# Linear attention and two MLPs: the first MLP layer by layer, its second layer by seven products

## The chip, the cores and the metric

The kernel runs on one core of a Trainium2 chip. The metric is the time of one execution on the device in microseconds; shown are the median of several runs and one profiled execution. The engines are TensorE (PE; its weight loads are shown apart as PEld), VectorE (DVE), ScalarE (ACT), GpSimd (POOL) and SyncE (SP), which issues all of the kernel's DMA transfers.

## The reference

All data are float32. Attention has 8 batches, 8 heads, 576 positions and heads of 64; its output, 4608 tokens by 512, goes through two MLPs (512 to 2048 to 512).

```python
def _attn_ref(q, k, v):
    q_s = q - np.max(q, axis=-1, keepdims=True)
    q_s = np.exp(q_s)
    q_s = q_s / (np.sum(q_s, axis=-1, keepdims=True) + 1e-09)
    k_s = k - np.max(k, axis=2, keepdims=True)
    k_s = np.exp(k_s)
    k_s = k_s / (np.sum(k_s, axis=2, keepdims=True) + 1e-09)
    kv = np.einsum('bhsd,bhse->bhde', k_s, v)
    return np.einsum('bhsd,bhde->bhse', q_s, kv)
# x = attention, as tokens by 512
# first MLP:  h = x @ w_in; x = np.maximum(0.01 * h, h) @ w_out
# second MLP: h = x @ w_in; out = (h / (1 + np.exp(-h))) @ w_out
```

## The kernel before, in words

**Precision.** TensorE multiplies in float32r. To keep accuracy each operand is split in a high part (a rounded copy, ScalarE) and a low part (the rest, VectorE, `sub`), and a product is three matmuls: high by high, high by low, low by high.

**Tiling.** Tokens go in 9 blocks `j` of 512 (`TB`), the inner dimension of an MLP in 16 row blocks `f` of 128. A unit of attention is one pair of heads and one block: 36 units `n`, four for each block. `k_task`, `v_task` and `q_task` load a unit, take the maxima and exponentials, form k times v in `kv` (L554, L555) and x for one quarter of the inner dimension (L690). k's maximum over positions needs a transpose, q's softmax another. Units below `DT` = 14 transpose on TensorE (L522, L528, L675, then a copy out of PSUM), later ones on VectorE in pieces of 32 by 32 (L498 to L514; 16 pieces for q, L665).

**First MLP.** Both layers run fused. `layer1` makes one row block of one block of tokens (12 matmuls of 512 columns, L723 to L725), `act` applies the leaky ReLU (L750) and splits the result into a g tile, and `layer2_all` adds its share to four accumulators in PSUM (12 matmuls, L782), which stay for a whole block. Both layers' weights are decoded by `split1` (two ScalarE and four VectorE instructions and a split for each piece) while the first two blocks run, and stay in SBUF. The first two blocks are done in halves (`chunks`).

**Second MLP.** It runs layer by layer, and each layer multiplies blocks of 2 by 2 with seven products in place of eight. A product is 12 matmuls of 256 columns. Layer 1 (`layer1_2`, L1005) does seven products per block of tokens and group `i` of four row blocks, `blocks` puts them together, `active` applies the SiLU, and the results go to DRAM (`gd`). Layer 2 (`layer2_2`, L1054) fetches them (`g_all`) and sums over the four groups in seven PSUM banks. Operands of a product are loaded, some are sums of others (`SUMS`), and each is split (`operand`: `fetch`, `sums`, `split2`). `weights1` and `weights2` do that with the weights, which `convert2` and `convert3` decoded and put into DRAM. x operands live in 12 buffers (`r_x`), seven for each set; the weights in 28.

**What sets the order.** The program is written by a planner (`Queues`): each task is a generator that offers its next instruction with an estimated cost and waits for buffers (`get`) and events (`wait`). The planner takes what can start first, and among equals the lowest rank. Every engine and SyncE's queue then run in that order and wait by semaphores.

**PSUM.** Eight banks: four accumulators (`pacc`), two for layer 1 (`r_h`), two for attention (`r_attn`). The second MLP takes all eight (`r_b`).

Of the kernel before, what the change touches and what calls it, by code (L numbers as in the profile page):

```python
# [202 lines left out]
def linear_attention_two_mlps(  # L203
# [37 lines left out]
    DT = 14  # L241
    NE = 7
    NX = 6
    FS = 6
    NU = 7
    NS = 8

# [8 lines left out]
    pacc = ctx.enter_context(tc.tile_pool(name="pacc", bufs=1, space=PSUM))  # L256
    ph = ctx.enter_context(tc.tile_pool(name="ph", bufs=2, space=PSUM))
# [24 lines left out]
    r_attn = Slots(qs, [lambda i=i: pa.tile([P, TB], F32, tag=f"a{i}", name="a") for i in range(2)])  # L282
# [3 lines left out]
    r_g = Slots(qs, gbuf)  # L286
    r_o = Slots(qs, [outp.tile([P, TB], F32, name=f"o{i}") for i in range(4)])
    r_x = Slots(qs)
    r_b = Slots(qs)
    r_k = ring(atp, [P, 640], F32, "k", 1)  # L290
    q_tiles = [atp.tile([P, TB], F32, name=f"q{i}") for i in range(3)]
    r_q = Slots(qs, q_tiles)
    kx_tile = atp.tile([P, 2, TB], F32, tag="kx", name="kx")
    r_kx = Slots(qs, [kx_tile[:, i] for i in range(2)])
    r_m = ring(sp, [P, 2, D], F32, "m1", 2)
# [12 lines left out]

    wtiles = {}
    spare = {}  # L310
# [43 lines left out]
    def parts_of(f):  # L354

        return ((0,), (1,)) if f < NE else ((0, 1),)

    def w_tag(f, os):
        return f"w{f}" if len(os) == 2 else f"w{f}_{os[0]}"

    def split1(f, os):

        if f == NF - 1:
            yield wait(("l2", 0, 3))
        if f > NF - NU:
            yield wait(("unit", NF - f))
        for e in range(NX):
            if f == NF - NU - e // 2:
                yield wait(("w", 0, 0, e), ("w", 0, 1, e))
        n = DM * len(os)  # L370
        raw = wp.tile([P, 2 * n], U32, tag=w_tag(f, os), name="r" + w_tag(f, os))
        for i, o in enumerate(os):
            yield from load_bits(raw[:, 2 * i * DM:2 * (i + 1) * DM], 0, o, f)
        if f < NX:

            if f // 2 not in spare:
                spare[f // 2] = wp.tile([P, 4, DM], F32, tag=f"w{NF - NU - f // 2}", name=f"t{f}")
            at = 2 * (f % 2) + os[0]
            t = spare[f // 2][:, at:at + len(os)].rearrange("p o n -> p (o n)")
        else:  # L380
            t = yield get(r_raw)
        yield from decode(raw, t[:, 0:n], n)
        w = wp.tile([P, len(os), 2, DM], F32R, tag=w_tag(f, os), name=w_tag(f, os))
        for i, o in enumerate(os):
            wtiles[0, o, f] = w[:, i]
        t2 = t[:, 0:n].rearrange("p (o n) -> p o n", n=DM)
        yield op(("A", a_(n)))
        copy("A", w[:, :, 0], t2)
        yield op(("V", v_tt(n)))
        sub("V", w[:, :, 1], t2, w[:, :, 0])  # L390
        if f >= NX:
            r_raw.put(t)
        for o in os:
            done(("w", 0, o, f))

    def convert2():

        yield wait(("l2", 2, NF - 1))
        for f in range(NF):
            raw = yield get(r_raw)  # L400
            bits = raw.bitcast(U32)
            yield from load_bits(bits, 1, 0, f)
# [4 lines left out]
            nc.sync.dma_start(out=w2d[f], in_=t[:, 0:DM])  # L407
            yield wait()
            r_raw.put(t)
            done(("w2", f))  # L410

    def convert3():

        yield wait(*(("w2", f) for f in range(NF)), ("l2", NB - 1, NF - 1))
        n = DM // 2
        for r in range(NF // 2):
            yield rank(step2(0, r, 0) - 4)
# [26 lines left out]
    def w_of(l, o, f):  # L444
        return wtiles[l, o, f].rearrange("p t (k m) -> p t k m", k=KD)


    kv = {}
    early = {}

    def early_tiles(n):

        if n not in early:
            w = wp.tile([P, 4 * DM], F32, tag=f"w{NF - n}", name=f"u{n}")
            early[n] = w[:, 0:640], w[:, 640:640 + 5 * NV], w[:, 1536:2048]
            nc.vector.memset(early[n][1].rearrange("p (c n) -> p c n", c=5)[:, :, 2 * D:], 1.0)
        return early[n]

    def k_task(n):

        b, j, p = units[n]
        first = 0 < n < NU
        if first:
            kf, vv, _ = early_tiles(n)
        else:
            kf, vv = (yield get(r_k)), vbuf
        ktile = kf
# [25 lines left out]
        if n >= DT:  # L493

            mt = yield get(r_m)
            mtf = mt.rearrange("p h d -> p (h d)")
            yield op(("V", 0.21))
            nc.vector.transpose(out=mtf, in_=m1f)  # L498
            yield op(("V", 0.21))
            nc.vector.tensor_reduce(  # L500
                out=sk[:, 0:4], in_=mtf.rearrange("p (a t) -> p a t", a=4), axis=AX.X, op=ALU.max
            )
            r_m.put(mt)
            for i in range(4):
                yield op(("V", 0.08))
                nc.vector.tensor_copy(out=sk[0:32, 4 + 4 * i:8 + 4 * i], in_=sk[32 * i:32 * i + 32, 0:4])
            yield op(("V", 0.09))
            nc.vector.tensor_reduce(
                out=sk[0:32, 20:24], in_=sk[0:32, 4:20].rearrange("p (i a) -> p a i", i=4),
                axis=AX.X, op=ALU.max, negate=True,  # L510
            )
            for i in range(4):
                yield op(("V", 0.21))
                nc.vector.transpose(  # L514
                    out=m1f[32 * i:32 * i + 32].rearrange("p (a d) -> p a d", a=4),
                    in_=sk[0:32, 20:24].unsqueeze(2).to_broadcast([32, 4, 32]),
                )
            nb = m1f
        else:
            pm = yield get(r_attn)  # L520
            yield op(("p", 0.12))
            nc.tensor.transpose(pm[:, 0:P], m1f, ident)  # L522
            r_m.put(m1)
            nm = small[n % 2]["k"][:, 0:1]
            yield op(("V", v_tt(128)))
            nc.vector.tensor_reduce(out=nm, in_=pm[:, 0:P], axis=AX.X, op=ALU.max, negate=True)
            yield op(("p", 0.12))
            nc.tensor.transpose(pm[:, P:2 * P], nm.to_broadcast([P, P]), ident)  # L528
            nb = pm[:, P:2 * P]
# [8 lines left out]
        if n >= DT:  # L538
            r_m.put(m1)
        else:  # L540
            r_attn.put(pm)
# [14 lines left out]
        if not first:  # L556
            r_k.put(ktile)
# [50 lines left out]
    def q_task(n):  # L608

        b, j, p = units[n]  # L610
        if n > DT:
            yield wait(("qt", n - 1))
# [545 lines left out]
```

## Time and profile before

| | |
|---|---|
| median of 3 runs | 1666.81 us (1665.66 to 1667.26) |
| profiled execution | 1667.91 us, its span 1666.1 us |
| busy: PE, PEld, DVE | 1623.2, 1447.5, 1132.0 us |
| busy: ACT, POOL | 766.4, 65.3 us |
| DMA | 194.71 MB, mean 117 GB/s |

Attention and the first MLP take the span up to about 945 us, the second MLP's first layer lasts until about 1300 us and its second to the end. A shown matmul lasts longer than the distance to the next one, as they overlap; a busy TensorE can so still be fed late. In groups of rows, "idle before" is the engine's idle time just before these instructions.

### The profile page before, as it was taken

How to read it: one execution, taken by the hardware profiler on the slowest of the kernel's cores; microseconds unless marked ns; L12 is line 12 of the kernel's file. 1: busy time of each engine (PE TensorE's matmuls, PEld its weight loads, DVE VectorE, ACT ScalarE, POOL GpSimd, SP SyncE). 2: the span in 40 equal slices, each digit the busy share in tenths (PEclk: the TensorE clock that was granted, in tenths of full speed). 3: DMA queues.
4: the chain of work that ended last, by engine and by line, in shares of the span. 5: the costliest groups of instructions: out<-in, count | busy, mean ns of one | idle time of the engine just before them, and what ended most of it. 6: DMA issues, size and time to landing. Idle time of an engine off the chain costs nothing.

```text
span 1666.1 us, 27003 instructions
## 1 busy us (share of the span) xinstructions
PE 1623.2 (97%) x10036; PEld 1447.5 (87%) x10036; DVE 1132.0 (68%) x2277; ACT 766.4 (46%) x1671; POOL 65.3 (4%) x74
## 2 busy tenths in 40 slices
PE   5899999999999999999999999999999999999999
PEld 3678888787877878887888999999999999999999
DVE  7988337657586784714124798888878877777775
ACT  5687454334353543423233545444446544444442
POOL 2200001101011010000000000000000000000000
PEclk9999999999999999999999999999999999999999
DMA  8741213113233321100021455555548644444442
GB/s 246 259 136 40 78 49 106 36 53 97 73 96 101 110 75 46 45 8 31 1 64 45 139 186 203 195 176 185 174 149 265 190 127 135 134 133 135 136 135 83
DMA packets 170883, 194.71 MB, mean 117 GB/s; under 512 B 53504, under 2 KB 120064, under 8 KB 170752
## 3 DMA queue, kind: packets, MB, share of 16 engines
q1 hardware_dynamic: 170752, 192.99, 37.5%
q8 instruction: 79, 1.29, 0.3%
q14 instruction: 52, 0.43, 0.1%
HBM read 122.68 MB, written 70.25 MB: 116 GB/s over the span
## 4 chain that ended last, share of the span: by engine, by line
PE 82%; DVE 11%; ACT 3%; DMA 2%; issue 1%; SPq 0%; POOL 0%; DVEq 0%; POOLq 0%; ACTq 0%
PE acc L782 18%; PE b L1054 11%; PE c L1054 11%; PE b L1005 11%; PE c L1005 10%; PE h L723 6%; PE h L724 6%; PE h L725 6%; DVE q L665 3%; PE a L690 1%; PE a L554 1%; ACT q L646 1%; DVE g L300 1%; DVE m L514 1%; DVE x L300 1%
## 5 line engine op out<-in xcount | busy, mean ns | idle before, releaser
L782 PE MATMUL acc<-g,w 128*128 128x512 f32 x1728 | 430.1, 395 | 0.4 <-ACT o L304 0.4
L782 PEld LDWEIGHTS acc<-g,w 128*128 128x128 f32 x1728 | 321.4, 188 | 71.7 <-issue 2.1
L300 DVE TENSOR_TENSOR g<-h,g 128x512 fp32r<-128x512 f32 x144 | 99.5, 691 | 243.5 <-ACT g L304 242.5
L723 PE MATMUL h<-x,w 128*128 128x512 f32 x576 | 234.7, 407 | 10.4 <-DVE g L300 7.9
L724 PE MATMUL h<-x,w 128*128 128x512 f32 x576 | 226.6, 393 | 1.6 <-DVE x L300 1.6
L725 PE MATMUL h<-x,w 128*128 128x512 f32 x576 | 226.2, 393 | 0.0
L304 ACT ACTIVATE g<-h 128x512 fp32r<-128x512 f32 x144 | 86.0, 597 | 149.3 <-PE acc L782 148.5
L750 ACT ACTIVATE h<-h 128x512 f32<-128x512 f32 x144 | 84.0, 583 | 143.4 <-PE h L725 140.2
L723 PEld LDWEIGHTS h<-x,w 128*128 128x128 f32 x576 | 108.8, 189 | 43.1 <-DVE g L300 14.1
L1054 PE MATMUL c<-s,x 128*128 128x256 f32 x1056 | 138.7, 283 | 0.4 <-DVE x L300 0.4
L1005 PE MATMUL b<-x,s 128*128 128x256 f32 x1056 | 137.0, 283 | 0.0
L1054 PEld LDWEIGHTS c<-s,x 128*128 128x128 f32 x1056 | 132.0, 192 | 0.6 <-DVE x L300 0.6
L1005 PE MATMUL c<-x,s 128*128 128x256 f32 x1008 | 131.8, 283 | 0.5 <-DVE o L940 0.5
L1005 PEld LDWEIGHTS b<-x,s 128*128 128x128 f32 x1056 | 131.3, 192 | 0.1
L724 PEld LDWEIGHTS h<-x,w 128*128 128x128 f32 x576 | 108.9, 189 | 25.7 <-DVE x L300 3.4
L725 PEld LDWEIGHTS h<-x,w 128*128 128x128 f32 x576 | 108.9, 189 | 23.9 <-DVE w L300 0.7
L1005 PEld LDWEIGHTS c<-x,s 128*128 128x128 f32 x1008 | 125.7, 192 | 0.7 <-DVE o L940 0.7
L1054 PE MATMUL b<-s,x 128*128 128x256 f32 x960 | 125.5, 283 | 0.0
L1054 PEld LDWEIGHTS b<-s,x 128*128 128x128 f32 x960 | 119.7, 192 | 0.0
L304 ACT ACTIVATE x<-x 128x512 fp32r<-128x512 f32 x110 | 69.4, 631 | 109.2 <-DMA x<-gd 76.7
L665 DVE STREAM_TRANSPOSE q<-q 32x128 f32<-32x128 f32 x352 | 106.4, 302 | 11.0 <-PE a L690 3.6
L646 ACT ACTIVATE q<-q,q 128x64 f32<-128x64 f32 x176 | 59.5, 342 | 51.8 <-DVE q L625 51.4
(228 smaller groups left out, 2308.2 us busy)
## 6 DMA issues: line engine op xcount, KB each, us to landing
x<-gd SPq DMA_DIRECT2D x92, 256.0 KB, 2.7
gd<-left SPq DMA_DIRECT2D x75, 256.0 KB, 2.6
gd<-o SPq DMA_DIRECT2D x41, 256.0 KB, 2.7
x2d<-o SPq DMA_DIRECT2D x34, 256.0 KB, 2.1
g<-gd SPq DMA_DIRECT2D x34, 256.0 KB, 2.8
rw<-in_moe_w_in_dram SPq DMA_DIRECT2D x16, 512.0 KB, 4.7
rw<-in_moe_w_out_dram SPq DMA_DIRECT2D x16, 512.0 KB, 5.8
raw<-in_moe_w_in_dram SPq DMA_DIRECT2D x16, 512.0 KB, 4.1
```

What stands on the lines that cost most here:

```text
L300: engines[e].tensor_tensor(out=out_, in0=a, in1=b.bitcast(F32), op=ALU.subtract)
L304: nc.scalar.activation(out=out_, in_=in_, func=ACTF.Copy)
L514: nc.vector.transpose(out=m1f[32 * i:32 * i + 32].rearrange("p (a d) -> p a d", a=4), in_=sk[0:32, 20:24].unsqueeze(2).to_broadcast([32, 4 ...
L646: nc.scalar.activation(out=x4[:, c, h], in_=q4[:, c, h], func=ACTF.Exp, bias=nq[:, at:at + 1], accum_out=sq[:, to:to + 1],)
L665: nc.vector.transpose(out=qT[32 * o:32 * o + 32].rearrange("p (c t) -> p c t", c=4)[:, :, 32 * i:32 * i + 32], in_=q4[32 * i:32 * i + 32, ...
L723: nc.tensor.matmul(h, lhsT=w[:, 0, kk], rhs=x[:, 0], start=kk == 0, stop=False)
L724: nc.tensor.matmul(h, lhsT=w[:, 0, kk], rhs=x[:, 1], start=False, stop=False)
L725: nc.tensor.matmul(h, lhsT=w[:, 1, kk], rhs=x[:, 0], start=False, stop=kk == KD - 1)
L750: nc.scalar.activation(out=h, in_=h, func=ACTF.Prelu, alpha=0.01)
L782: nc.tensor.matmul(a, lhsT=lhsT, rhs=rhs, start=f == first and i == 0, stop=f == last - 1 and i == 2)
L1005: nc.tensor.matmul(bank[:, r * HB:(r + 1) * HB], lhsT=w4[:, a, r, k], rhs=x3[:, b, k], start=n == 0, stop=n == 5,)
L1054: nc.tensor.matmul(bank[:, m * HB:(m + 1) * HB], lhsT=g[:, a, at:at + P], rhs=w[:, b, r * HB:(r + 1) * HB], start=i + m + n == 0, stop=i = ...
```

## The change

- The first MLP runs layer by layer as well. `layer0` makes layer 1 of all nine blocks; `act` now writes the leaky ReLU's result to SBUF, subtracts in even row blocks the first half of the tokens from the second (an operand of the products), and stores the block in DRAM (`gd1`).
- Its second layer is the same function as the second MLP's second layer (`layer_k(1)`): seven products, weights and x swapped as stationary and moving operand, results to `x2d` by `store1`.
- `w_out` of the first MLP is no longer decoded at the start by `split1` but later by `convert1`, into DRAM; `weights1` makes its operands. `convert2` and `convert3` start later.
- All units transpose on TensorE; VectorE's transposes are gone.
- Six sets of buffers for k and v (they take the room of weights that come later), six for q; four PSUM banks for attention and four for layer 1; 16 buffers `r_o`.

```diff
-    DT = 14
-    NE = 7
-    NX = 6
-    NU = 7
+    NU = 8
+    NH = 4
+    NO = 16
...
-    r_attn = Slots(qs, [... for i in range(2)])
-    r_h = ring(ph, [P, TB], F32, "h", 2)
+    r_attn = Slots(qs, [... for i in range(4)])
+    r_h = Slots(qs, [... for i in range(NH)])
...
+    def convert1():
+        yield wait(("l1", 1, NF - 1))
+        yield from convert(0, 1, w1d, "w1", lambda f: step(3, 0) + 4 * f)
+
     def convert2():
-        yield wait(("l2", 2, NF - 1))
...
+        yield wait(*(("w1", f) for f in range(NF)))
+        yield from convert(1, 0, w2d, "w2", lambda f: step2(1, f // 3, 0) - 4)
...
-        yield wait(*(("w2", f) for f in range(NF)), ("l2", NB - 1, NF - 1))
+        yield wait(*(("w2", f) for f in range(NF)), ("p", 1, NB - 2, NG - 1, 1))
...
-        if n >= DT:
-            qT = yield get(r_q)
-            done(("qt", n))
-            for i in range(4):
-                for o in range(4):
-                    yield op(("V", 0.2))
-                    nc.vector.transpose(...)
-            r_q.put(qt)
-        else:
...
+        yield wait(*([("kvs", n)] if NP <= n and b is not None else []), *([("xm", n - 2)] if n > 1 else []))
+        pq = yield get(r_attn)
+        yield op(("p", 0.45))
+        for c in range(4):
+            nc.tensor.transpose(pq[:, c * P:(c + 1) * P], qx[:, c * P:(c + 1) * P], ident)
...
+    def act(j, f, h):
+        o = yield get(r_o)
         yield op(("A", a_(TB)))
-        nc.scalar.activation(out=h, in_=h, func=ACTF.Prelu, alpha=0.01)
...
-        yield op(("A", a_(TB)))
-        copy("A", g[:, 0], h)
-        yield op(("V", v_tt(TB)))
-        sub("V", g[:, 1], h, g[:, 0])
+        nc.scalar.activation(out=o, in_=h, func=ACTF.Prelu, alpha=0.01)
+        r_h.put(h)
+        i, r, b = f // 4, f % 4 // 2, f % 2
+        if not b:
+            yield op(("V", v_tt(HB)))
+            nc.vector.tensor_tensor(out=o[:, HB:TB], in0=o[:, HB:TB], in1=o[:, 0:HB], op=ALU.subtract)
         yield op(("D", 0.73))
+        nc.sync.dma_start(
+            out=gd1[j][i, 2 * b:2 * b + 2, :, r * HB:(r + 1) * HB].rearrange("c p n -> p c n"),
+            in_=o.rearrange("p (c n) -> p c n", c=2),
+        )
...
-    def layer2_all():
...
-                    pairs = [(w[:, 0, m], g[:, 0]), (w[:, 0, m], g[:, 1]), (w[:, 1, m], g[:, 0])]
...
+    def weights(l, i, srcs, kind, order):
+        def give(c):
+            n = 7 * i + c - 1
+            if l == 1:
+                m = n - (NW - NF)
+                yield wait(("kv", B * NP - 1) if m < 0 else ("l1", NB - 1, m))
+                return w_room(n, [P, 2, DM], F32R, "a")
+            yield wait(("p", l - 1, NB - 1, i, c))
+            return slot[("w", l - 1, i), c]
...
+    def layer_k(l):
         for j in range(NB):
             for i in range(NG):
                 for c in ORDER:
...
+                    s, x = (w, g) if l == 1 else (g, w)
...
+    def layers():
+        yield from layer_k(1)
+        yield from layer2()
+        yield from layer_k(3)
```

Three places show how the order moves. The first is TensorE at the start, behind the fourth row block of layer 1 for block 0; before, the next row block's weights are `w_0_725`, now `w_713`. Before:

```order
L782 MATMUL acc_566<-g,w_1_477 128x512 x3
L782 MATMUL acc_574<-g,w_1_477 128x512 x3
L782 MATMUL acc_550<-g_539,w_1_541 128x512 x3
L675 MATMUL a<-ident,o_130 128x128 x4
L522 MATMUL a<-ident,m_553 128x128
L782 MATMUL acc_559<-g_539,w_1_541 128x512 x3
L782 MATMUL acc_566<-g_539,w_1_541 128x512 x3
L782 MATMUL acc_574<-g_539,w_1_541 128x512 x3
L690 MATMUL a<-u_156,kv_105 128x64
```

And now:

```order
L475 MATMUL a<-ident,m_502 128x128
L603 MATMUL a<-ident,o_168 128x128 x4
L503 MATMUL a<-u_171,kx 128x129 x4
L504 MATMUL a<-u_171,u_170 128x129
L481 MATMUL a<-ident,k_148 128x128
L618 MATMUL a<-uq_184,kv_112 128x64
L603 MATMUL a<-ident,o_154 128x128 x4
L618 MATMUL a<-uq_184,kv_116 128x448
L618 MATMUL a<-uq_182,kv_113 128x64
L503 MATMUL a<-u_173,kx 128x129 x4
```

The second layer's products (L782), which stood between attention's instructions, are gone from here, and attention of units 4 to 7 (L603 the transposes of q, L503 and L504 k times v, L618 x) stands alone.

The second place is a unit of a later block, before on VectorE, where q's transposes (L665) are mixed with layer 1's splits (`g<-h,g`):

```order
L665 STREAM_TRANSPOSE q_132<-q_134 32x4x32
L300 TENSOR_TENSOR g<-h,g 128x512
L300 TENSOR_TENSOR x_115<-a,x_115 128x4x80
L665 STREAM_TRANSPOSE q_132<-q_134 32x4x32 x6
L486 TENSOR_TENSOR o_131<-k 128x256
```

Now on TensorE, between layer 1's products (L646 to L648):

```order
L603 MATMUL a<-ident,o_155 128x128 x4
L503 MATMUL a<-u_179,kx 128x129 x4
L504 MATMUL a<-u_179,u_178 128x129
L646 MATMUL h<-x_121,w_342 128x512
L647 MATMUL h<-x_121,w_342 128x512
L648 MATMUL h<-x_121,w_342 128x512
L603 MATMUL a<-ident,o_168 128x128 x4
```

Transposes left VectorE and stand among TensorE's products.

The third place is VectorE at the end of the first MLP. L819 forms sums, L294 splits; `a` are weights of the next layer, `x` and `g` buffers of x sets; the `x` and `g` rows here end the last set but one of the old layer:

```order
L294 TENSOR_TENSOR x_122<-o_162,x_122 128x512
L819 TENSOR_TENSOR o_153<-a_3466,a_3470 128x512
L294 TENSOR_TENSOR g<-o_163,g 128x512
L819 TENSOR_TENSOR o_166<-a_3470,a_3469 128x512
L819 TENSOR_TENSOR o_154<-o_166,a_3466 128x512
L819 TENSOR_TENSOR o_167<-a_3467,o_154 128x512
L294 TENSOR_TENSOR a_3466<-a_3466 128x512
L294 TENSOR_TENSOR a_3467<-a_3467 128x512
L294 TENSOR_TENSOR a_3468<-o_167,a_3468 128x512
```

Eleven instructions on weights (nine shown with the rows of x) stand before the last set; before, the weights of the first MLP's second layer needed none here.

## Rows read from the trace of the kernel before

**Rows 1.** the page, part 1: busy time, share of the span, instructions of each engine
```profile
PE 1623.2 (97%) x10036; PEld 1447.5 (87%) x10036; DVE 1132.0 (68%) x2277; ACT 766.4 (46%) x1671; POOL 65.3 (4%) x74
```

**Rows 2.** windows of three later stretches; columns: stretch, its length, each engine's busy time
```profile
800.00:920.00 120.00, 120.00 (x531) 99.38 (x531) 35.05 (x54) 38.85 (x68) 0.00 (x0) 1.00 0.13 40
1000.00:1300.00 300.00, 300.00 (x2502) 300.00 (x2501) 248.96 (x410) 146.30 (x250) 0.00 (x0) 1.00 0.59 196
1350.00:1650.00 300.00, 300.00 (x2502) 300.00 (x2501) 218.35 (x348) 132.47 (x214) 0.00 (x0) 1.00 0.45 128
```

**Rows 3.** windows of the first 800 us, same columns
```profile
0.00:100.00 100.00, 74.46 (x311) 52.97 (x312) 87.69 (x201) 62.24 (x123) 19.57 (x28) 0.97 0.82 255
100.00:250.00 150.00, 149.59 (x689) 122.12 (x689) 86.48 (x149) 91.74 (x231) 4.58 (x4) 1.00 0.19 54
250.00:800.00 550.00, 537.69 (x2396) 434.85 (x2395) 337.58 (x925) 225.94 (x674) 41.12 (x42) 1.00 0.23 66
```

**Rows 4.** TensorE's waits, first 100 us: total us, times, longest
```profile
PE a L522 <- DVE m L492: 7.0, 4, 4.9
```

**Rows 5.** TensorE's waits, 250 to 800 us
```profile
PE h L723 <- DVE g L300: 7.9, 11, 1.6
PE a L554 <- ACT kx L544: 2.8, 4, 1.4
```

**Rows 6.** windows at two handovers and in a dense stretch of DMA
```profile
990.00:1000.00 10.00, 9.49 (x79) 9.29 (x78) 9.44 (x17) 3.69 (x6) 0.00 (x0) 1.00 0.48 177
1290.00:1300.00 10.00, 10.00 (x85) 10.00 (x85) 9.69 (x17) 7.07 (x13) 0.00 (x0) 1.00 0.97 313
1310.00:1320.00 10.00, 9.59 (x79) 9.31 (x78) 9.97 (x18) 5.84 (x10) 0.00 (x0) 1.00 0.40 109
```

**Rows 7.** timeline of TensorE around 230 us: start, us, engine, line, operation, count
```profile
224.86 0.81 PE L690 MATMUL a<-q,kv 128*128 128x384 f32 x2
225.50 0.27 PE L528 MATMUL a<-ident,k 128*128 128x128 f32 x1
225.53 3.02 PE L782 MATMUL acc<-g,w 128*128 128x512 f32 x12
228.38 0.39 PE L723 MATMUL h<-x,w 128*128 128x512 f32 x1
...
230.42 1.05 PE L554 MATMUL a<-vb,kx 128*128 128x129 f32 x8
...
231.82 0.50 PE L723 MATMUL h<-x,w 128*128 128x512 f32 x1
...
234.68 0.60 PE L675 MATMUL a<-ident,o 128*128 128x128 f32 x4
235.04 0.95 PE L782 MATMUL acc<-g,w 128*128 128x512 f32 x3
235.82 0.39 PE L723 MATMUL h<-x,w 128*128 128x512 f32 x1
```

**Rows 8.** VectorE by form, 4 to 60 us: count, busy, mean ns, idle before
```profile
L486 DVE TENSOR_TENSOR o<-u 128x256 f32<-128x256 f32 x5 | 3.8, 754 | 0.0
...
L625 DVE TENSOR_REDUCE q<-u 128x8 f32<-128x512 f32 x5 | 3.4, 673 | 0.0
...
L526 DVE TENSOR_REDUCE k<-a 128x1 f32<-128x128 f32 x5 | 1.4, 281 | 0.0
...
L653 DVE RECIPROCAL rq<-rq 128x8 f32<-128x8 f32 x5 | 1.0, 203 | 0.2
```

**Rows 9.** window 4 to 60 us, instructions on weight pieces' tile t alone
```profile
4.00:60.00 56.00, 25.46 (x40) 12.27 (x20) 0.97 0.86 257
```

**Rows 10.** TensorE by line, 0 to 150 us: count, busy, mean ns, idle before
```profile
L782 PE MATMUL acc<-g,w 128*128 128x512 f32 x158 | 40.8, 400 | 0.4 <-ACT o L304 0.4
L723 PE MATMUL h<-x,w 128*128 128x512 f32 x68 | 29.3, 431 | 2.5 <-ACT x L699 2.5
```

More of the change, by code (lines that the diff above doesn't have):

```diff
@@ L352, in decode, with split1, convert @@
         )
[L354 to L379, printed above, removed]
-        else:
[L381 to L396, printed above, removed]
-        yield wait(("l2", 2, NF - 1))
+    def split1(f):
+        room = NW - NF + f
+        raw = w_room(room, [P, 2 * DM], U32, "rw")
+        yield from load_bits(raw, 0, 0, f)
+        t = yield get(r_o)
+        yield from decode(raw, t, DM)
+        w = w_room(room, [P, 2, DM], F32R, "w")
+        wtiles[f] = w
+        yield op(("A", a_(DM)))
+        copy("A", w[:, 0], t)
+        yield op(("V", v_tt(DM)))
+        sub("V", w[:, 1], t, w[:, 0])
+        r_o.put(t)
+        done(("w", f))
+    def convert(l, o, dst, name, r):
         for f in range(NF):
+            yield rank(r(f))
             raw = yield get(r_raw)
             bits = raw.bitcast(U32)
-            yield from load_bits(bits, 1, 0, f)
+            yield from load_bits(bits, l, o, f)
             t = yield get(r_raw)
@@ L442, in convert3, with w_of @@
             done(("w2c", r))
[L444 to L457, printed above, removed]
+    def w_of(f):
+        return wtiles[f].rearrange("p t (k m) -> p t k m", k=KD)
+    kv, of = {}, {}
+    sets = []
+    for n in range(6):
+        k_, v_ = (w_room(2 * n + i, [P, 2 * DM], F32, "u") for i in range(2))
+        sets.append((k_[:, 0:640], v_[:, 0:5 * NV]))
+    r_kv = Slots(qs, sets)
+    r_q = Slots(qs)
+    for n in range(3):
+        t = gp.tile([P, 2, TB], F32, tag=f"g{n}", name=f"uq{n}")
+        r_q.add(t[:, 0], t[:, 1])
     def k_task(n):
         b, j, p = units[n]
[L462 to L467, printed above, removed]
+        if n >= NU:
+            yield wait(("kvs", n - NU))
+        of[n] = yield get(r_kv)
+        kf, vv = of[n]
+        done(("set", n))
         heads = slice(2 * p, 2 * p + 2)
@@ L555, in k_task @@
         nc.tensor.matmul(pk[:, 0:NV], lhsT=k1, rhs=vv[0:SR, 4, :], start=False, stop=True)
-        if not first:
-            r_k.put(ktile)
+        r_kv.put(of.pop(n))
         r_kx.put(kx)
         done(("kv", n))
-        if n >= NKV - NP:
-            yield wait(("xm", n - NKV + NP))
-        rk = small[n % 2]["k"][:, 1:2]
+        rk = small[n % NU]["k"][:, 1:2]
         yield op(("V", 0.15))
@@ L693, in q_task @@
             if e == P:
-                if not 0 < n < NU:
-                    r_q.put(qT)
+                r_q.put(qT)
                 done(("xm", n))
@@ L794, in earlier @@
[L794 to L816 removed]
+                yield from layer0(j, f)
@@ L817, in finish @@
         yield wait()
         r_o.put(o)
-        if last == NF:
-            done(("x2", j, m))
+        done(("gd1", j, f))
     HB = TB // 2
@@ L833, in linear_attention_two_mlps @@
     KEPT = (1, 2, 4, 5)
+    KEPT1 = (1, 5, 2, 3)
     slot = {}
@@ L983, in blocks, with layer2 @@
         spawn(r, give(2, 1, u))
[L985 to L988 removed]
+    def layer2():
         for j in range(NB):
             for i in range(NG):
[L991 to L992 removed]
+                at = step2(2, j, i)
+                spawn(at - 2, blocks((2, j, i), at - 2, lambda a, b, t, j=j, i=i: active(j, i, a, b, t)))
                 for c in ORDER:
@@ L1035, in keep @@
         done(("gd", j, i, c))
-    def layer2_2():
-        yield wait("layer 1")
+    def layer_k(l):
         for j in range(NB):
@@ L1074, in later @@
     def later():
-        yield wait(("unit", len(units) - 1))
+        yield wait(*(("unit", n) for n in range(len(units))))
+        r_x.add(*gbuf)
         r_x.add(atp.tile([P, 2, TB], F32R, tag="kx", name="xs"))
-        r_o.add(*q_tiles)
+        r_b.add(*(pa.tile([P, TB], F32, tag=f"a{i}", name="b") for i in range(4)))
     units = [(j if j < B else None, j, p) for j in range(NB) for p in range(NP)]
@@ L1085, in step2 @@
     def step2(layer, j, i):
-        return NB * NF + ((layer * NB + j) * NG + i) * 2
+        return NB * NF + (((layer - 1) * NB + j) * NG + i) * 2
     with tc.manual_schedule():
-        nc.vector.memset(vbuf.rearrange("p (c n) -> p c n", c=5)[:, :, 2 * D:], 1.0)
+        nc.vector.memset(ones, 1.0)
         make_identity(nc, ident)
-        nc.scalar.activation(out=sk[:, 0:1], in_=vbuf[:, 2 * D:NV], func=ACTF.Exp)
+        nc.scalar.activation(out=small[0]["k"][:, 0:1], in_=ones, func=ACTF.Exp)
+        for _, t in sets:
+            nc.gpsimd.memset(t.rearrange("p (c n) -> p c n", c=5)[:, :, 2 * D:], 1.0)
         for t in kvbuf:
```

357 lines of the change are left out of this document (127 added, 230 removed), and 1 row of the table SUMS.

## The prediction

> **What bounds the kernel now.** I read the page first, for who is busy; then the windows, stage by stage; then what TensorE waited for; then, where it waited, the engine it waited for, by instruction; last the timeline of TensorE around a transpose. TensorE is busy 97% of the span and VectorE 68% [rows 1]. From 800 us on nothing holds TensorE up: its busy time fills the windows [rows 2]. So in two thirds of the span a change counts only by the number of matmuls times their spacing. The spacing is window over count: 120 us / 531 = 0.226 us for a matmul of 512 columns, 300 / 2502 = 0.120 us for one of 256. (One shown duration, 0.4 us, is longer, since matmuls overlap.)
>
> The start is different. In the first 100 us TensorE is busy 74.5 us and VectorE 87.7 [rows 3], and the first wait of TensorE's list is for VectorE [rows 4]. The start is VectorE's. From 250 to 800 us TensorE misses 12.3 us in 550, between 100 and 250 us only 0.4 in 150 [rows 3]. The two stretches differ in how the transposes are done: units up to 13 use TensorE, later ones VectorE, and the chief wait of the later stretch is a product of layer 1 that waits until VectorE has emptied a PSUM bank [rows 5].
>
> **The seven products.** The first MLP's second layer loses 9 x 16 x 12 = 1728 matmuls of 512 columns and gets 9 x 4 x 7 x 12 = 3024 of 256. 1728 x 0.226 = 390.5 us; 3024 x 0.120 = 362.9 us (by 300/2502, 362.6); the term is **-28 us**. The second MLP's two layers run in that form without a gap [rows 2], so a stage of this kind can be fed. What feeds it: per block VectorE does 4 x 10 instructions for operands and 7 for the sums of products, as the last layer does, whose windows show it busy 218 of 300 us [rows 2]. The layer also writes every result of layer 1 to DRAM and reads it back; the same traffic exists beside the last layer (128 GB/s there [rows 2], against 313 in a dense stretch [rows 6]), so I put it at nothing. On SyncE's queue the 144 stores wait for ScalarE and VectorE, and attention's loads stand behind them; six sets of buffers let those loads start units ahead, which hides it. If that cover goes, a unit comes late, and that is rival (b). The 32 decodes that move into layer 1 (four instructions of VectorE and two of ScalarE each) lie beside TensorE's work, where VectorE was busy 338 us of 550 [rows 3] and now loses its transposes: nothing, unless VectorE fills up there.
>
> The Trainium skill, "TensorE: Matmul & The Clock Gate", section "Back-to-back issue gap", gives 262 cycles for 256 columns and 518 for 512, at full clock 0.109 and 0.216 us; by that the term would be an estimated -43 us. This trace disagrees for float32r operands (0.120 and 0.226), and its numbers decide.
>
> **Transposes to TensorE.** 22 more units transpose q there (four matmuls against the identity), 18 more transpose the maximum and its broadcast (one each). Four for q: 0.36 us until the next matmul starts, and the three that follow take 0.78 us where 3 x 0.226 = 0.68 is usual: 0.46 us. One for k: 0.03, and the twelve behind it take 2.85 instead of 2.71: about 0.16 [rows 7]. 22 x 0.46 + 36 x 0.16 = **+15.9 us**. From the other side, 124 single transposes at the 0.27 us that one shows would be 33; I stay with the spacing, since it is what the neighbours lose. Not below 22 x 0.36 + 36 x 0.03 = 9.
>
> The Trainium skill, same page, "Part 4: PE-mode transpose", tells of about 275 ns for one transpose inside a kernel. 124 of those would be an estimated 34 us. The row shows that length too, but the next matmul does not wait for its end.
>
> **The start.** The order says what changes: between the fourth and the fifth row block of layer 1, TensorE used to have the second layer's products; now it has only attention of units 4 to 7. VectorE must do 8 units and 5 weight pieces before the fifth. A unit is 0.75, four of about 0.68, four of about 0.28 and four of at most 0.20 us = 5.3 us [rows 8]; a weight piece, five instructions, 25.46 / 8 = 3.2 us [rows 9]; 8 x 5.3 + 5 x 3.2 = 58 us, which with the 4 us before its first work and some 3 of idling ends near 65. From there 11 more pieces take 35 us, to 100, while TensorE has 8 products (8 x 2.71 = 22 us) in hand, then ten that follow the weights, to about 117, then ten of block 1 (27 us) and beside them attention of four units. One unit costs TensorE about 1.4 us for k times v, about 0.6 for x [rows 7] and, from above, 0.46 + 2 x 0.16 for transposes: 2.7 us or a little over. So block 1 ends at 117 + 27 + 4 x 2.7 = 155 us, with 32 x 2.71 + 12 x 2.7 = 119 done. Lost: 36 us. Before, on the same count, 158 + 3 x 68 = 362 matmuls [rows 10] and nine units, 362 x 0.226 + 9 x 2.7 = 106 us, were done in the first 150: lost 44. The term is **-8 us**, with bounds 0 (the long gap costs what the weights of the second layer cost before) and -15 (VectorE without idling, and units 8 to 11 inside the gaps).
>
> **The middle.** With VectorE's transposes and its subtraction per row block gone from layer 1, and four banks instead of two, the wait for a bank should go. What is late next is the attention chain: a unit comes every 4 x 2.71 + 2.7 = 13.5 us of TensorE's time, instead of with twice as many products between, and has five places in TensorE's order instead of two; each waits for ScalarE or VectorE, and the matmuls queued behind it wait with it. By the stretch with TensorE transposes 28 units would lose 28/6 x 0.4 = 2 us in place of 12.3; by the longest wait on ScalarE there [rows 5], 1.4 us each, 39. I take 5, near the first: **-7 us**, bounds -10 and +27.
>
> **The handovers.** Two old ones stay: at 990 and at 1310 us, where all operands change, TensorE lost 0.5 and 0.4 us [rows 6]. One is new, and the one into the second MLP changes. Into the products of the first MLP: half of the weights' 28 operands wait for layer 1's last row blocks, and the second x set gets its buffers only when layer 1 ends; it needs a load, then VectorE's 10 instructions behind the last weights' 11, 21 x 0.67 [rows 8] = 14 us where 10 us of products are there to cover it: 4 us. Into the second MLP: the order puts x of the next layer and two sets of weights (33 instructions) between the last three sets of the old one; from the end of the first set to the end of the last VectorE has 68 instructions, 68 x 0.67 = 46 us if they do not overlap (218/348 = 0.63 each where they do [rows 2]: 43), while TensorE has about 38 us of work: 5 us or more. The old handover at 1310 had VectorE busy 9.7 and 9.97 of 10 us [rows 6], so there is no slack for the 16 sums (11 us) that these weights need and those did not. **+8 us**, bounds +1 and +25.
>
> **Sum.** The profiled execution took 1667.9 us (span 1666.1 and 1.8 around it). 1667.9 - 28 + 15.9 - 8 - 7 + 8 = 1648.8. The median of the runs, 1666.8, is 1.1 us under the profiled one: **1647.7 us**.
>
> **Rivals.** (a) *The gaps close entirely*: start -15, middle -10, handovers +1: 1667.9 - 28 + 15.9 - 15 - 10 + 1 - 1.1 = 1631. For it: no wait between 100 and 250 us; against: twice the units per microsecond.
> (b) *Attention starves TensorE*, the slower side. Place: layer 1 from block 2 on; price: 1.4 us for each of 28 units, +27 instead of -7, 1682. For it: ScalarE waits 1.4 us behind and has eight exponentials per unit in a row; against: 0.4 us lost in six units of just this form. It decides from 0.8 us per unit on: 28 x 0.8 = 22 is 17 more than the 5 I take, which makes 1665.
> (c) *The handovers stall*: a set of x for the next layer takes 7 of the 12 buffers while the old layer still needs two sets, and each load is then in the open: +25 instead of +8, 1665. For it: VectorE has no slack at 1310 us; against: 0.4 us lost there.
> (d) *Transposes cost their full length*: +33 instead of 15.9, 1665. Against: the starts in the timeline.
> That the change does not do what it says is excluded by the order: the matmuls are there in the new number.
>
> **How the numbers follow.** This kernel's runs differ by 0.1%, and 0.2% (3.3 us) is about what can be told: faster is under 1663.5, slower above 1670. My forecast 0.50 (own range 1638 to 1662), (a) 0.20, (b) 0.15, (c) 0.09, (d) 0.06. Faster: 0.50 + 0.20 and most of a half of (c) and (d), 0.78. Same: the upper halves of those and a little of (b), 0.07. Slower: the rest of (b), 0.15. The range leaves out half of (a) below and most of (b) above: 1629 to 1671.
>
> **What would show it.** In the new profile: 0.120 us spacing from layer 2 of the first MLP to the end, three stages of about 363 us; transposes in layer 1 whose next matmul starts 0.03 to 0.1 us later; TensorE nearly without layer products between some 43 and 65 us; under 10 us missing from 150 us to the end of layer 1; some microseconds missing behind each of the two handovers, with VectorE full. I am wrong if TensorE waits for ScalarE in every unit (b), or if a handover shows more than 10 us.

## The result and the profile after

The changed kernel takes **1651.03 us** (median of 4 runs, 1649.95 to 1652.46), the kernel before in the same session 1667.03: a ratio of 0.9902 with a 95% interval from 0.9885 to 0.9919, or 16 us less where 19 were forecast. The profiled execution took 1649.95 us, its span 1648.2.

The page of the changed kernel, part 1 (busy time, share, instructions) and the row of the granted clock in part 2 (40 slices of the span), against [rows 1]:

```profile
PE 1602.6 (97%) x11456; PEld 1504.0 (91%) x11456; DVE 1185.9 (72%) x2170; ACT 849.4 (52%) x1824; POOL 41.7 (3%) x56
...
PEclk9999999999999999999997899999999999999999
```

One place stands out: in two slices, at about 865 to 948 us, the clock is not full. Windows of the changed kernel, columns as in [rows 2, 3]:

```profile
0.00:100.00 100.00, 77.37 (x345) 57.83 (x346) 87.78 (x201) 63.01 (x125) 19.87 (x36) 1.00 0.83 237
100.00:250.00 150.00, 150.00 (x763) 122.86 (x763) 92.68 (x272) 111.84 (x413) 13.71 (x13) 1.00 0.64 183
250.00:528.00 278.00, 278.00 (x1278) 227.50 (x1277) 127.55 (x275) 153.37 (x425) 8.08 (x7) 1.00 0.57 179
528.00:800.00 272.00, 272.00 (x2268) 271.96 (x2267) 212.42 (x345) 130.50 (x213) 0.00 (x0) 1.00 0.50 148
840.00:940.00 100.00, 81.31 (x616) 80.62 (x615) 86.44 (x141) 48.70 (x82) 0.00 (x0) 0.86 0.50 152
```

From 100 to 800 us TensorE misses nothing, where [rows 3] missed 12.7 us; VectorE has 220 us of work between 100 and 528 us instead of 424 between 100 and 800. Behind 800 us, where [rows 2] had no gap, there is one now. TensorE's waits behind 540 us (total us, times, longest), but for one of 0.5 us:

```profile
PE b L931 <- DVE x L294: 8.1, 1, 8.1
PE b L881 <- DVE o L819: 6.5, 1, 6.5
PE b L931 <- DVE g L294: 4.1, 1, 4.1
...
```

L931 is the product of the two second layers, L881 that of the second MLP's first. All three lie around the second handover. Timeline of TensorE there:

```profile
879.27 2.71 PE L931 MATMUL b<-x,a 128*128 128x256 f32 x11 [8.12 <-DVE x L294]
...
895.64 2.71 PE L931 MATMUL b<-g,a 128*128 128x256 f32 x11 [4.06 <-DVE g L294]
...
929.18 2.93 PE L881 MATMUL b<-xs,a 128*128 128x256 f32 x12 [6.51 <-DVE o L819]
```

The first two gaps stand before the last two operand sets of the first MLP, the third before a product of the new layer whose PSUM bank VectorE has not emptied. Eleven matmuls behind the first start within 2.52 us, 0.23 us apart, nearly twice the usual 0.120: the clock has fallen to its lower level. Windows of 10 us show it as 0.68 and 0.74:

```profile
870.00:880.00 10.00, 1.89 (x13) 1.68 (x12) 9.90 (x17) 5.13 (x9) 0.00 (x0) 0.68 0.32 89
...
920.00:930.00 10.00, 3.49 (x27) 3.29 (x26) 9.70 (x16) 7.17 (x11) 0.00 (x0) 0.74 0.18 52
```

The Trainium skill, "TensorE: Matmul & The Clock Gate", section "HAM oscillation — how this bites in real kernels", says that a pause between bursts of matmuls is paid a second time, because the next burst starts at half the clock; the trace agrees, with 0.23 us against 0.120. In the stage 26.4 us are lost and 18.7 of them are waits; the wider distances behind the three gaps make 7.2 us of the rest.

**How the 16 us come about.** For every kind of TensorE instruction I took the median distance to the next start times the count (net time); what the distances exceed that is lost. (A transpose's delay of the matmul behind it counts as lost.)

| | before | after | difference |
|---|---|---|---|
| net: the first MLP's second layer | 392.3 | 362.9 | -29.4 |
| net: transposes | 7.3 | 18.4 | +11.1 |
| net: all else | 1192.3 | 1191.5 | -0.8 |
| lost, first 100 us | 37.0 | 28.9 | -8.1 |
| lost, 100 us to the end of attention | 27.0 | 9.5 | -17.5 |
| lost, later | 1.4 | 27.5 | +26.1 |
| ahead of the first, behind the last start | 8.9 | 9.4 | +0.5 |
| span | 1666.1 | 1648.2 | -17.9 |

### The profile page after: what moved, and what is told of

It is laid out like the page before. It is cut to its first block, busy times and chain, and to the rows that moved or that the text cites. A ratio compares the mean times of both kernels' runs of the same rounds, so it can differ in the third digit from the quotient of the medians.

```text
span 1648.2 us, 30726 instructions
## 1 busy us (share of the span) xinstructions
PE 1602.6 (97%) x11456; PEld 1504.0 (91%) x11456; DVE 1185.9 (72%) x2170; ACT 849.4 (52%) x1824; POOL 41.7 (3%) x56
## 4 chain that ended last, share of the span: by engine, by line
PE 92%; DVE 5%; DMA 1%; issue 1%; ACT 1%; SPq 0%; DVEq 0%; ACTq 0%
PE b L931 22%; PE h L931 21%; PE b L881 10%; PE h L881 10%; PE h L646 8%; PE h L648 8%; PE h L647 8%; PE a L618 2%; PE a L503 2%; DVE o L819 1%; DVE a L294 1%; PE a L603 1%; PE a L504 1%; DVE x L294 0%; DMA raw<-in_moe_w_out_dram 0%
## 5 line engine op out<-in xcount | busy, mean ns | idle before, releaser
L646 PE MATMUL h<-x,w 128*128 128x512 f32 x576 | 237.1, 412 | 3.2 <-ACT w L298 2.5
L648 PE MATMUL h<-x,w 128*128 128x512 f32 x576 | 225.5, 391 | 1.2 <-DVE w L294 1.2
L819 DVE TENSOR_TENSOR o<-o,h 128x512 f32<-128x512 f32 x190 | 127.5, 686 | 50.3 <-PE h L931 20.2
L819 DVE TENSOR_TENSOR o<-o,b 128x512 f32<-128x512 f32 x188 | 126.3, 686 | 45.7 <-PE b L931 18.6
L931 PE MATMUL b<-a,x 128*128 128x256 f32 x1104 | 141.6, 283 | 0.0
L294 DVE TENSOR_TENSOR x<-x 128x512 fp32r<-128x512 f32 x211 | 138.7, 685 | 2.4
L298 ACT ACTIVATE x<-o 128x512 fp32r<-128x512 f32 x166 | 103.7, 631 | 65.8 <-DVE o L819 46.3
L931 PE MATMUL b<-x,a 128*128 128x256 f32 x1008 | 129.5, 286 | 8.1 <-DVE x L294 8.1
L931 PEld LDWEIGHTS b<-a,x 128*128 128x128 f32 x1104 | 136.5, 192 | 0.3 <-DVE x L294 0.2
L646 PEld LDWEIGHTS h<-x,w 128*128 128x128 f32 x576 | 108.4, 188 | 29.7 <-ACT w L298 3.3
L881 PE MATMUL b<-x,a 128*128 128x256 f32 x1044 | 134.8, 285 | 0.0
L931 PEld LDWEIGHTS b<-x,a 128*128 128x128 f32 x1008 | 125.9, 195 | 8.3 <-DVE x L294 8.3
L648 PEld LDWEIGHTS h<-x,w 128*128 128x128 f32 x576 | 108.1, 188 | 25.7 <-DVE w L294 2.5
L881 PE MATMUL h<-x,a 128*128 128x256 f32 x1020 | 130.9, 283 | 0.0
L881 PEld LDWEIGHTS b<-x,a 128*128 128x128 f32 x1044 | 130.1, 194 | 0.0
L931 PE MATMUL h<-x,a 128*128 128x256 f32 x1008 | 126.8, 283 | 0.0
L881 PEld LDWEIGHTS h<-x,a 128*128 128x128 f32 x1020 | 126.1, 192 | 0.0
```

The costliest lines, as they stand in the source:

```text
L294: engines[e].tensor_tensor(out=out_, in0=a, in1=b.bitcast(F32), op=ALU.subtract)
L298: nc.scalar.activation(out=out_, in_=in_, func=ACTF.Copy)
L646: nc.tensor.matmul(h, lhsT=w[:, 0, kk], rhs=x[:, 0], start=kk == 0, stop=False)
L648: nc.tensor.matmul(h, lhsT=w[:, 1, kk], rhs=x[:, 0], start=False, stop=kk == KD - 1)
L819: nc.vector.tensor_tensor(out=o, in0=a, in1=b, op=alu)
L881: nc.tensor.matmul(bank[:, r * HB:(r + 1) * HB], lhsT=w4[:, a, r, k], rhs=x3[:, b, k], start=n == 0, stop=n == 5,)
```

## The experiments

Each kernel is the changed one (1651.0) with the edit shown; most were run once, beside the kernel before on the same chip (1667.1 to 1668.6).

A single time holds a part that no edit here touches. E1 to E4, E6, E8 and E9 run the same instructions in the same order on every engine in the first 100 us as the changed kernel, yet their traces lose 28.9 to 33.7 us in the first 100 us. So the gaps are judged by the lost time from 840 to 960 us, 26.4 us in the changed kernel; E8, with the same order there, lost 24.7, so 2 us are about what can be told.

### Who holds up the middle: VectorE's transposes or the banks

Two parts of the change could have taken the waits of [rows 5] away. E7 takes two of attention's and two of layer 1's banks away again; E8 puts q's transposes of units 14 on back on VectorE.

```diff
E7
-    NH = 4
+    NH = 2
-    r_attn = Slots(qs, [... for i in range(4)])
+    r_attn = Slots(qs, [... for i in range(2)])
E8
+        if n >= DT:   # DT = 14
+            ... nc.vector.transpose(...)   # 16 of 32x32
+        else:
```

> The changed kernel with two PSUM banks for attention and two for layer 1, as before; the four others wait unused for the products. For the middle (100 to 528 us, where TensorE waits 0.0 us). Theory A (the waits of before came from VectorE, whose transposes held up the emptying of banks): still under 2 us of waits, time within 2 us of 1651. Theory B (the number of banks took the waits away): 8 to 12 us of waits come back, 1660 us.

> The changed kernel with q's transposes on VectorE again from unit 14 on, banks as changed. TensorE has 22 x 0.46 = 10 us less to do. Theory A: TensorE's waits in the middle come back, about 0.5 us per unit, 10 us, so the time is about the same, 1648 to 1654 us. Theory B: no waits, the 10 us are gained, 1641 us: then it was the banks and the split that went out of layer 1.

E7: 1655.52 us. A window of it (the columns as above):

```profile
250.00:530.00 280.00, 280.00 (x1296) 228.48 (x1295) 133.08 (x295) 158.59 (x444) 8.66 (x8) 1.00 0.57 179
```

With two banks each TensorE still misses nothing there, nor from 100 to 250 us; lost time of both stretches is 10.0 us (9.5 with four). So theory A's waits came true and its time did not: E7 is 4.5 us longer, and its trace loses more chiefly at the start, 35.9 us against 28.9. As the changed kernel's own order lost up to 33.7 there in other runs, the banks are worth between 2 and 7 us at the start. E8: 1651.25 us. Its window and TensorE's waits from 100 to 528 us:

```profile
250.00:530.00 280.00, 275.24 (x1223) 222.82 (x1222) 198.66 (x523) 148.23 (x445) 12.82 (x10) 0.99 0.56 176
```
```profile
PE a L634 <- DVE x L295: 2.9, 2, 2.0
PE a L634 <- issue: 1.9, 1, 1.9
PE a L476 <- DVE m L473: 1.7, 3, 1.1
```

The waits are back, in attention instead of at a bank, and lost time is 21.9 us in place of 9.5. The stage ends at 530.7 us instead of 528.2: 12.3 us more lost, 2.5 later, so the transposes that left TensorE were worth some 10 us, 22 units x 0.45. So q's transposes on VectorE make TensorE wait in the middle, even with four banks; moving them costs 10 us of TensorE's time and saves 12. These 12 are not the whole of the table's 17.5: k's transposes and the split behind layer 1 left VectorE too and were not put back, so where the other 5 come from is not shown.

### What makes the gaps of the second handover

VectorE of the changed kernel in the first gap (x and g are operands, a the second MLP's weights):

```profile
869.73 1.29 DVE L819 TENSOR_TENSOR o<-a,a 128x512 f32<-128x512 f32 x2
...
872.39 1.28 DVE L294 TENSOR_TENSOR a<-a 128x512 fp32r<-128x512 f32 x2
873.60 0.68 DVE L819 TENSOR_TENSOR o<-x,x 128x512 f32<-128x512 f32 x1
...
876.73 1.89 DVE L294 TENSOR_TENSOR a<-o,a 128x512 fp32r<-128x512 f32 x3
878.54 0.68 DVE L294 TENSOR_TENSOR x<-x 128x512 fp32r<-128x512 f32 x1
```

The split that TensorE waits for (878.54) stands behind eleven instructions on the next layer's weights. That is the first theory: VectorE has too much work that is not yet due. SyncE's queue shows two more:

```profile
862.32 0.36 SPq L713 DMA_DIRECT2D x<-x2d  x1
862.77 1.47 SPq L713 DMA_DIRECT2D a<-w2d  x2
865.20 0.33 SPq L713 DMA_DIRECT2D x<-gda  x1
866.75 0.33 SPq L713 DMA_DIRECT2D g<-gda  x1
868.08 1.76 SPq L713 DMA_DIRECT2D x<-gda  x2
871.08 13.58 SPq L713 DMA_DIRECT2D a<-w2d  x4
```

The set's four loads (from `gda`) are issued only from 865.2 to some 869 us, about 1.4 us apart, as TensorE frees the buffers of the set before, since the next layer's first x set (from `x2d`) already holds seven of twelve: the second theory, rival (c). And the set after it waits in the queue behind weights' loads that take 13.58 us to be issued: the third.

**E1 to E3.** E1 asks for the x set one step ahead of its use in place of ten (steps are ranks of the planner; seven products count two); E2 for the weights two steps ahead in place of eight; E3 gives the weights' 16 sums to GpSimd.

```diff
E1
-            r = step2(2, j, 0) - 10
+            r = step2(2, j, 0) - (10 if j else 1)
E2
-        ... step2(l, 0, i) - 8, order, srcs, give)
+        ... step2(l, 0, i) - (2 if l == 2 else 8), order, srcs, give)
E3
+            if key[:2] == ("w", 2):
+                nc.gpsimd.tensor_tensor(out=t, in0=ax, in1=ay, op=alu)
...
```

> Only the first x set of the second MLP is made later: its rank goes behind the first MLP's last sets, so that those keep the 12 buffers. Theory 1 (VectorE's order: instructions on the next layer's weights stand before the last sets' splits): the weights still stand there, the gaps of 8.1 and 4.1 us at 871 and 892 us stay, about 1648 us or more. Theory 2 (buffers: the next layer's x holds 7 of 12, so loads of the last two sets start late): both gaps go and the clock stays up, 1635 to 1640 us; a new gap of at most 5 us before the first product of the next layer.

> Only the weights of the second MLP's first layer get a later rank (2 steps ahead instead of 8). Theory 1: VectorE finishes the old layer's last sets first, the first two gaps shrink to under 4 us together, and the third (6.5 us at 922) stays or grows as the weights come later: 1637 to 1645 us. Theory 2: the last two sets still lack buffers, both gaps stay: about 1650 us.

> Only the 16 sums of the second MLP's first weights move from VectorE to GpSimd (about 1.2 us each there). Theory 1: VectorE has 11 us less in the 60 us of the handover, all three gaps shrink, 1635 to 1642 us. Theory 2: the first two gaps stay, the third goes at best: 1644 us or more. GpSimd's length could also delay the weights: then the second and third gaps grow.

E1: 1658.56 us. Its timeline of TensorE:

```profile
874.53 3.01 PE L931 MATMUL b<-x,a 128*128 128x256 f32 x23 [0.45 <-DVE x L294]
...
888.41 2.71 PE L931 MATMUL b<-g,a 128*128 128x256 f32 x11 [3.14 <-DVE g L294]
...
922.11 2.71 PE L881 MATMUL h<-x,a 128*128 128x256 f32 x11 [23.78 <-DVE x L294]
```

The first gap falls from 8.1 to 0.5 us although the weights keep their places: the x set's early place opens it. (The edit moves the set's claim of buffers and its eleven VectorE instructions together; E5 changes the buffers alone.) But a set asked for so late costs 23.8 us at its own use. E2: 1663.0; the first gap halves and the second stays:

```profile
878.84 2.72 PE L931 MATMUL b<-x,a 128*128 128x256 f32 x11 [4.37 <-DVE x L294]
...
895.42 2.72 PE L931 MATMUL b<-g,a 128*128 128x256 f32 x11 [4.15 <-DVE g L294]
```

and the late weights make waits of 13.6 us (four times) in the new layer. So by E2 the first gap has two parts: 3.7 us that the weights' instructions add, and 4.4 that stay without them; that late loads make these is not shown by E2 itself. E3: 1653.45, and the gaps grow to 12.2 and, in two waits, 5.3 us, while the third shrinks; 26.1 us are lost, as before. A sum took 1.61 us on GpSimd where I had put 1.3, against 0.69 on VectorE. As the expectation allowed, such sums can delay the weights, so E3 does not tell what fewer sums alone would bring.

**E4 to E6.** E4 lets the decode of the last weights wait until the new layer has run its first block. E5 adds to E4 two operand buffers (14; two buffers `r_o` fewer). E6 adds to E4 that the seven operands of the second MLP's first weights are made when those are decoded, so that no sums are left for the handover.

```diff
E4
-        yield wait(*(("w2", f) ...), ("p", 1, NB - 2, NG - 1, 1))
+        yield wait(*(("w2", f) ...), ("p", 2, 0, NG - 1, 1))
E5
-    NO = 16
+    NO = 14
...
+        r_x.add(sp.tile([P, 2, TB], F32R, tag="kvb", name="xk"))
+        r_x.add(xp.tile([P, 2, TB], F32R, name="xe"))
E6
+    w2a = tc.dram_tile([NF // 2, P, 7, DM // 2], F32, name="w2a")
...
+        srcs = {c: w2a[2 * i:2 * i + 2, :, c - 1]... for c in range(1, 8)}
+        yield from weights(2, i, srcs, "", ORDER)
```

> Only the decode of the last weights starts later, after the second MLP's first block. Theory 1: VectorE loses some 10 instructions (6 us) between the second and the third gap; the third gap (6.5 us) mostly goes, the first (8.1) stays: about 1643 us. Theory 2 says the same of the first two gaps; of the third it says nothing.

> The late decode of the last weights (as in the run before that gained by it) and 14 buffers for x sets instead of 12: one is the room of attention's k-times-v tiles, one is won by 14 sum buffers instead of 16. Theory 2 (buffers): of the two gaps that were left, 7.9 and 3.7 us, most goes, under 5 us together, and with the clock 1630 to 1636 us. Theory 1 (VectorE's load): both stay, about 1643 us.

> The late decode of the last weights, and the 16 sums of the second MLP's first weights made when these are decoded, beside layer 1, instead of at the handover; 12 buffers. Theory 1 (VectorE's load and order): VectorE has 11 us less at the handover, the two gaps shrink to under 5 us, 1630 to 1637 us. Theory 2 (buffers): both stay, about 1643 us.

E4: 1643.74; the third gap is gone, the first two stay (7.9 and 3.7 us). The decode, beside the new layer's first sums on VectorE, was its cause; lost time falls from 26.4 to 17.0 us. E5: 1640.44, with these waits behind 540 us:

```profile
PE b L932 <- DVE x L295: 7.0, 2, 5.5
PE b L882 <- DVE o L820: 3.7, 1, 3.7
```

Two buffers take 4.6 us off the first two gaps (11.6 to 7.0), though a wait for a bank comes back, and 14.2 us are lost: less than theory 2 asked. TensorE reaches the first gap at 874.8 us in E4 and 874.9 in E5; the first loads of the two sets behind the gaps are issued at 868.79 and 889.19 us in E4, at 866.06 and 882.97 in E5. That the old sets' loads wait for buffers is so shown. Three sets at once (in use, next, and the new layer's) would need 21. E6: 1645.27, gaps of 6.5 and 5.9 us, 17.5 us lost: lighter work on VectorE alone does not help, though E6 also loads seven operands of a group in place of four.

**E9 to E11.** E9 is E4 with the weights' loads on GpSimd's queue; E10 is E5 with the same; E11 is E5 with the x set asked for five steps ahead.

```diff
E9, E10
-        nc.sync.dma_start(
+        (nc.gpsimd if key[:2] == ("w", 2) else nc.sync).dma_start(
E11
+            r = step2(2, j, 0) - (10 if j else 5)
```

> The kernel with the last weights' decode moved behind the second handover (1643.7 us there, waits of 7.9 and 3.7 us left) and, besides, the loads of the second MLP's first weights issued on GpSimd's queue instead of SyncE's; order and buffers are the same. Queue theory (loads of the last operand set of the layer before stand on SyncE's queue behind four weight loads that must wait for the old weights to be read, 13.5 us for four): the two gaps shrink to under 5 us together, 1636 to 1640 us. VectorE theory (what delays the last splits is the order and the load on VectorE, not the loads): gaps of 10 to 13 us stay, 1643 to 1645 us.

> The same with two more operand buffers (14 instead of 12; with them alone 1640.4 us and 10.7 us of waits left). If queue and buffers are two causes that add up: under 3 us of waits, 1632 to 1637 us. If the queue is nothing: 1639 to 1642 us.

> 14 operand buffers and the last weights' decode moved, loads on SyncE's queue as in the changed kernel; the first operand set of the second MLP is now made five products' steps ahead of its use instead of ten (one step ahead moved a gap of 23.8 us to the next layer's first product). If what is too early at ten is the set's eleven VectorE instructions among the last splits: both gaps shrink under 4 us together, and no new gap of over 3 us comes at the first product, 1634 to 1638 us. If the work is only shifted: the waits stay at 9 to 13 us in sum, wherever they stand, 1639 to 1643 us.

E9: 1645.31, gaps of 7.3 and 3.7 us; E10: 1640.25, against 1640.44 without the queue. The first load of the last set, in E4, in E9 and in E5:

```profile
889.19 0.33 SPq L713 DMA_DIRECT2D g<-gda  x1
...
888.74 0.32 SPq L713 DMA_DIRECT2D g<-gda  x1
...
882.97 0.33 SPq L714 DMA_DIRECT2D x<-gda  x1
```

The third theory falls: with the weights' loads on another queue this load comes only 0.45 us earlier, with two more buffers 6.2 us (2.4 of them by the shorter first gap). E11: 1643.52 and 16.2 us lost, as if the work were only shifted, with smaller waits at more places (and one of 0.5 us):

```profile
PE b L882 <- DVE o L820: 4.3, 1, 4.3
PE h L882 <- DVE g L295: 2.0, 1, 2.0
PE h L932 <- DVE x L295: 1.9, 1, 1.9
PE b L882 <- DVE xe L295: 1.1, 1, 1.1
...
```

With the buffers in hand the old layer's gaps shrink to 2.4 us, but the new set's splits now come only while TensorE already waits for them (g at 899.65 us, xe at 902.66), and the wait for a bank is longer.

**E12** is all that pointed somewhere: E5, E6 and E11, and the weights asked for five steps ahead.

```diff
+        ... step2(l, 0, i) - (5 if l == 2 else 8), order, srcs, give)
```

> All that the runs so far point to, in one kernel: decode of the last weights behind the second handover, 14 operand buffers, the second MLP's first weights' seven operands made when they are decoded (12 sums less on VectorE at the handover), and the order spread: the second MLP's first operand set and its weights asked for five steps ahead instead of ten and eight, so that in VectorE's queue the last two sets of the layer before come ahead of them. Theory A (a gap is the sum of two terms: operands that can only be loaded once the set before has released its buffers, 4.4 us, and VectorE's queue of next-layer work ahead of their splits, 3.5 to 4 us; with 14 buffers and this order both go): the waits after the first 540 us sum to under 4 us, 1632 to 1636 us. Theory B (VectorE simply has more work in these 100 us than it can do, whatever the order; it is 89% busy there): 8 to 11 us of waits stay, if at other places, 1638 to 1642 us.

**1628.78 us** (median of 5 runs, 1625.76 to 1631.26), ratio to the kernel before 0.9764, interval 0.9748 to 0.9781: it beats both kernels, and falls below the 1632 to 1636 that theory A gave. Its waits behind 540 us but for one of 0.2 us, and VectorE at the place of the first gap:

```profile
PE b L908 <- DVE o L846: 2.4, 1, 2.4
...
```
```profile
872.78 0.69 DVE L846 TENSOR_TENSOR o<-x,x 128x512 f32<-128x512 f32 x1 [0.93 <-DMA x<-gda]
...
874.71 2.49 DVE L295 TENSOR_TENSOR x<-x 128x512 fp32r<-128x512 f32 x4
...
878.93 1.28 DVE L295 TENSOR_TENSOR a<-a 128x512 fp32r<-128x512 f32 x2
881.14 1.29 DVE L846 TENSOR_TENSOR o<-g 128x512 f32<-128x512 f32 x2 [0.93 <-DMA g<-x2d]
```

The old layer's set comes first now, the new weights and the new x set (`g`, from `x2d`) follow, and VectorE even idles for loads. From 840 to 940 us it is busy 88% and the granted clock stays at 1.00 (behind the wait of 2.4 us, from 950 to 960 us, it is 0.83):

```profile
840.00:940.00 100.00, 100.00 (x835) 100.00 (x835) 88.39 (x143) 57.95 (x98) 0.00 (x0) 1.00 0.63 204
```

So theory B falls for this kernel: VectorE does 143 instructions in these 100 us, the changed kernel 141, and TensorE misses nothing. But of the handover's own work sums are gone here and the decode comes later, so it is not shown that the order alone would do. Lost time of the stage is 4.1 us instead of 26.4. How much of the last step is the order and how much the sums that are gone was not separated: E11 with the weights' old order and all sums lost 16.2 us there, E6 with the sums gone but twelve buffers and the old order 17.5.

## Why the prediction was right, point by point

The sign, the range and nearly the size were right, but that the size came so near is luck: the sum hides two errors, of some 15 us in the middle and 18 at the handovers, that cancel.

- **Seven products, -28 us:** right, -29.4. 3024 matmuls at 0.120 us, no gap inside the stage except at its end.
- **The start, -8 us:** -8.1 of lost time, but one trace does not bear the size: kernels with the same order at the start lose 28.9 to 33.7 us, so against the one trace of the kernel before (37.0) the gain is 3.3 to 8.1. Over 150 us it is 32.1 against 38.7, where 36 (in 155 us) against 44 were forecast. The first step is right, the fifth row block was put at 65 us. TensorE between the fourth and it:

```profile
63.08 0.60 PE L603 MATMUL a<-ident,o 128*128 128x128 f32 x4
65.75 0.50 PE L646 MATMUL h<-x,w 128*128 128x512 f32 x1 [2.08 <-ACT w L298]
```

  The later steps are not: row blocks that follow the weights were to lose more until 117 us, but from 70 to 100 us TensorE loses 0.1 us. The banks, which the term does not count, have a part in it (E7). Most of what differs between kernels of the same order is the granted clock; the changed kernel and E4:

```profile
50.00:60.00 10.00, 7.30 (x39) 4.75 (x39) 8.60 (x29) 9.28 (x21) 3.37 (x4) 1.00 0.99 309
...
50.00:60.00 10.00, 8.63 (x34) 6.28 (x35) 6.57 (x22) 6.95 (x16) 3.19 (x3) 0.66 0.84 267
```

- **Transposes, +15.9 us:** right in its prices. For q E8 gives 0.45 us, 0.46 was forecast. For k the timeline of the changed kernel shows 0.02 us to the next start and 0.32 in place of 0.23 for the next step, some 0.12 us against 0.16 (the same at 27 such places):

```profile
199.81 0.27 PE L475 MATMUL a<-ident,m 128*128 128x128 f32 x1
199.83 0.47 PE L646 MATMUL h<-x,w 128*128 128x512 f32 x1
200.15 0.39 PE L647 MATMUL h<-x,w 128*128 128x512 f32 x1
```

- **The middle, -7 us:** far too small. The mechanism is the one named, VectorE's transposes, for 12 of the 17.5 us (E8), but the banks, named beside them, have no part in it (E7), and the 5 us that attention was to go on losing did not come: no wait in 428 us. That is -12.7 in waits; the rest of the lost time that went is distances between matmuls stretched without a wait, which the forecast had not counted. In the account transposes and middle come to +11.1 - 17.5 = -6.4 us, against +8.9 forecast. Rival (b) is refuted by the same windows.
- **The handovers, +8 us:** the step that failed. The first was put at 4 us and costs nothing: L931 starts at 528.17 us right behind L648. The second was put at "5 us or more" and costs 26.4. Its arithmetic counted VectorE's instructions against TensorE's work (46 us against 38) as if they came in the order of need. What the runs show in its place is first rival (c), which I gave 0.09: the x set of the next layer holds seven of twelve buffers while the old layer needs two more sets (E1, E5). Besides, the weights' instructions stand ahead of the last splits (E2), and a third term that no rival had, the decode of the last weights, falls into the same stretch (E4, 9.4 us of lost time). The rise of 26.1 us lies just above the upper bound of 25, and by the prediction's own sign, a handover of more than 10 us, it was wrong here. Missing from every term was the clock, 7.2 us of the 26.4.

E12 mends this one term: its lost time at the handover is 26.4 - 4.1 = 22.3 us smaller, and it takes 1651.0 - 1628.8 = 22.2 us less than the changed kernel.

## What to carry to other kernels

Where one layer follows another, count not only the instructions but what each holds: a task of the next layer that claims buffers early starves the last tasks of this one, and the wait turns up as a full engine. Relieving that engine alone changed nothing here (E6), two more buffers closed a part (E5), and claims, order and work changed together closed nearly all of it (E12); which of them could be left out is open. Count a gap of TensorE as long as these (3.1 to 23.8 us) twice: once for the wait, once for the slower clock behind it. And before a single run is read, look at what the same order gives elsewhere: here the start alone moved by 5 us.

## What the runs showed of the hardware

I had expected a wait to cost its own length. In E1, 12 us into its gap of 23.8 us, the granted clock of a window of 10 us is at the lower level throughout, and 11 matmuls behind the gap take 2.71 us as behind the gaps of 3.1 to 8.1 us (behind E11's wait of 2.0 us 11 take 1.68):

```profile
910.00:920.00 10.00, 0.00 (x0) 0.00 (x0) 9.96 (x17) 3.61 (x7) 0.00 (x0) 0.50 0.01 2
```

At the start the granted clock differs between executions of the same instructions in the same order: from 50 to 60 us it is 1.00 in the changed kernel and E1, 0.66 in E2, E3, E4 and E9.

A sum of 128 x 512 took 1.61 us on GpSimd, 2.3 times VectorE's 0.69; products of that shape whose second operand is only eight numbers wide (L596 of the changed kernel) took 1.10 there.
